# A planned attention and mixer kernel: low parts and sign products from GpSimd to VectorE, with a new order of steps

## The chip, the cores and the metric

The kernel runs on one core of a Trainium2 chip. The metric is the device time of one execution in microseconds. Three runs of the kernel before gave 651.3, 648.9 and 648.49 us; their median is 648.9 us. Engines are named as the profile names them: PE is TensorE, DVE is VectorE, ACT is ScalarE, POOL is GpSimd, and SP is the engine that issues every DMA here.

## The reference

Four batches of 768 tokens go through three stages. The first is a gated linear attention with 8 heads of 48 channels:

```
for t in range(S):
    state = alpha[:, :, t, :, None] * state + einsum('bhd,bhe->bhde', k[:, :, t], v[:, :, t])
    y[:, :, t] = einsum('bhd,bhde->bhe', q[:, :, t], state)
```

The second mixes tokens and channels (`x` is the attention's output, 384 channels wide):

```
theta = x @ w_theta
y = w_tok_r @ (x * cos(theta)) + w_tok_i @ (x * sin(theta))     # over tokens, each batch
u = x + y
x = u + maximum(u @ w_ch, 0)
```

The third is a gated feed-forward: `h = relu(x @ w_in)`, one half of `h` is normalised and mixed over tokens by `w_spatial`, the other half multiplies it, and the result goes through `w_out`. Five of the six weight matrices come as 64-bit floats; `w_spatial` is 32-bit.

## The kernel before

**Units.** A batch is cut into 6 units of 128 tokens, 24 units in all, numbered u = 0 to 23. A unit goes through a chain over four engines: VectorE scans the decays (`att_scan`, two scans and a reciprocal, L451 to L455) and scales keys and queries (`att_kh` L463, `att_qh` L470); PE multiplies them (`att_a` L482, `att_k` L499, `att_u` L515); VectorE masks (`att_mask` L489) and carries the state from half to half (`att_s` L524, `att_t` L537); SP moves the state to another tile by DMA (`move_s` L529); PE forms the output (`att_y` L549), ScalarE copies it (`att_x`), PE transposes it (`tr_p` L568), and the product with `w_theta` follows in two parts (`th_p`, L591 and L594). VectorE reduces the angle (`th_r` L602), ScalarE takes sine and cosine, VectorE multiplies by x (`z_m` L620). Then comes the token mixing: `tokmix(u, m, ri)`, six steps of six matmuls for each unit (L652), which sum over the batch's six units in PSUM.

**High and low parts.** Matmuls of the mixer run on a reduced float type, so that each operand is split into a high part (a rounded copy, made by ScalarE: `z_h` L624, `high` L355 and L357) and a low part, the difference (`z_l` L629 for the activations, `low` L364 for weights, L366 for scaled ones). Three products, high by high, high by low and low by high, make one full product.

**Weight pieces.** The 64-bit weights are turned into 32-bit floats on the chip, in pieces of 128 x 384. `conv` plans the steps of one piece: SP loads it (`raw_f64` L313, two buffers), ScalarE or VectorE takes the sign apart (`sgn` L319 or L321, then `sign` L341), VectorE joins the two halves of the bits (`bits` L329, `join` L336), ScalarE takes the magnitude (`mag` L344), the product with the sign follows (`mul` L349), then `high` and `low`. There are 54 pieces, numbered n: 0 to 2 are `w_theta`, 3 to 26 the two token weights (four pieces for each unit of a batch), 27 to 29 `w_ch`, 30 to 53 the third stage. So the token weights are converted during the first batch, and stay.

**Which engine.** Three numbers share this work between VectorE and GpSimd. `MULP = 3` gives every third piece's sign product to GpSimd (14 of the 42 pieces that have one), `LOP = 2` gives it the low parts of two pieces in four (26, w_theta left out), and `ZLP = 6` the activation low parts of the first six units. Besides, GpSimd only clears four tiles at the start and takes 24 small powers in the third stage.

**Order.** No engine's order is written by hand. Each piece of work is a step with an engine, a cost, predecessors and the buffers that it takes; `latest()` gives it a time, worked back from due times of the token mixing, plus an offset by the step's name (`OFF`, and `OFF0` and `OFF3` for units of the first and last batch). `order()` places the steps on engines by these times, and the program is emitted in the order that comes out, for all engines. Each engine then runs its own steps strictly in that order; SP does too, so a DMA whose buffer is not yet free holds up all DMAs behind it. PSUM has three rotating buffers for all of these products.

Of the kernel before, what the change touches and what calls it, by code (L numbers as in the profile page):

```python
# [40 lines left out]
TH = S // 2  # L41
T0 = 512
OFF = {
# [6 lines left out]
    "sgn": -23.49, "mag": 39.17, "mul": -72.53, "high": -59.59, "low": 17.5, "v": -1.84, "vr": 121.16, "vb": 138.25,  # L50
    "vw": -48.53, "vm": 45.12, "vh": -80.17, "vl": 72.49, "g_u": -21.79, "g_r": -32.74, "g_s": -40.03, "g_m": -104.87,
    "g_h": -88.37, "g_l": 5.15, "o_p": -6.46, "o_e": 26.76, "x2h": 78.95, "x2l": 23.69, "x2": -32.84,
}
SLACK = 1.5
START = 30.0
# [1 line left out]
CHT = 10.6  # L57
CHD = 3.0
LEAD = 1
LOP = 2  # L60
RAWB = 2
OFF0 = {
# [5 lines left out]
}  # L68
OFF3 = {
# [5 lines left out]
}  # L75
SGA = 3
MULP = 3
ZLP = 6
QHB = 2
AMB = 2  # L80
SSB = 2
# [137 lines left out]
def attention_mixer_kernel(  # L219
# [150 lines left out]
    def conv(src, part, key, tiles=(), scale=None):  # L370

        n = len(cvs)
        c = {"src": src, "a": src.shape[1], "part": part, "scale": scale}
        cvs.append(c)
        pool = scale is None and n % 4 < LOP
        c["eng"] = nc.gpsimd if pool else nc.vector
        before = [raws[-1]] if raws else []
        raw, sg, cv = ("raw", RAWB, n), ("sg", 2, n), ("cv", 2, n)
        if src.dtype == I64:
            k0 = step(OFF["raw"], "dma", 1.6, raw_f64, n, after=before, tiles=[raw, *tiles])  # L380
            raws.append(k0)
            k1 = step(OFF["sgn"], *(("act", 0.54) if n % 4 < SGA else ("dve*", 0.27)), sgn, n, after=[k0], tiles=[raw, sg])
            k2 = step(OFF["bits"], "dve*", 0.27, bits, n, after=[k0], tiles=[raw, cv])
            k2 = step(OFF["bits"], "dve*", 0.47, join, n, after=[k2], tiles=[raw, cv])
            k3 = step(OFF["sgn"], "act", 0.52, sign, n, after=[k1], tiles=[sg])
            c["mulp"] = n % MULP == MULP - 1
            k2 = step(OFF["mag"], "act", 0.42, mag, n, after=[k2], tiles=[cv])
            k = step(OFF["mul"], *(("pool*", 0.96) if c["mulp"] else ("dve*", 0.47)), mul, n, after=[k3, k2], tiles=[sg, cv])
        else:
            k = step(OFF["raw"], "dma", 0.8, raw_f32, n, after=before, tiles=[cv, *tiles])  # L390
            raws.append(k)
        k = step(OFF["high"], "act", 0.41, high, n, after=[k], tiles=[cv, *tiles])
        k = step(OFF["low"], *(("pool*", 0.96) if pool else ("dve*", 0.47)), low, n, after=[k], tiles=[cv, *tiles])
        conv_done.setdefault(key, []).append(k)

    wt = {}
# [351 lines left out]
    x2 = {}  # L748
# [144 lines left out]
    for u in range(NU):  # L893
# [21 lines left out]
        ksc = at("sc", "dve*", 2.7, att_scan, after=[kal, prev("att_scan")], tiles=[al, rt])  # L915
        kkh = at("kh", "dve*", 0.6, att_kh, after=[ksc, kqk], tiles=[qk, rt, kh])
        kqh = at("q", "dve*", 0.6, att_qh, after=[ksc, kqk], tiles=[qk, al, qh])
        ka = at("A", "pe", 1.15, att_a, after=[kkh, kqh], tiles=[kh, qh, ps("a")])
        km = at("m", "dve", 0.6, att_mask, after=[ka, ("load_cst",)], tiles=[ps("a"), am])
        k = at("K", "pe", 0.4, att_k, after=[kkh, ("load_cst",)], tiles=[kh, ps("k")])  # L920
        kkt = at("kt", "act", 0.42, att_kt, after=[k], tiles=[ps("k"), kt])
# [2 lines left out]
        kms = []  # L924
        ktx = ("att_t", u - 1, 1) if i else None
        for c in range(2):
# [5 lines left out]
                kms.append(at(f"ms{c}", "dma", 0.3, move_s, c, after=[k, prev("att_y", back=2)], tiles=[*ss, sd]))  # L932
            if not (final and c):
                ktx = at(f"t{c}", "dve", 0.27, att_t, c, after=[k, ku], tiles=[ps("u", c), ("tmp", 1, (u, c)), *ss])
        ky = at("Y", "pe", 1.3, att_y, after=[kqh, km, kvt, *kms], tiles=[qh, am, sd, vd, ps("y")])
        kx = at("x", "act", 0.375, att_x, after=[ky], tiles=[ps("y"), x])
        kp = at("P", "pe", 0.33, tr_p, after=[kx, prev("th_p", 1)], tiles=[x, ps("t")])
        kxh = at("xh", "act", 0.375, tr_h, after=[kp], tiles=[ps("t"), xh])
        kxt = at("xt", "act", 0.375, tr_t, after=[kp], tiles=[ps("t"), xt])
        kxl = at("xl", "dve", 0.46, tr_l, after=[kxh], tiles=[xh, ps("t")])  # L940
# [188 lines left out]
```

## Time and profile before

| what | value |
|---|---|
| median of three runs | 648.9 us |
| profiled execution, its own time | 648.46 us |
| its span, first to last instruction | 646.7 us |
| PE busy | 600.4 us, 93% |
| DVE busy | 431.3 us, 67% |
| ACT busy | 283.4 us, 44% |
| POOL busy | 79.2 us, 12%, 78 instructions |
| DMA, share of 16 engines' span | 31.6% |

1.8 us of the profiled execution lie outside the span. Busy shares are averages over very different stages: PE is busy in 1, 4, 7 and 6 tenths of the page's first four slices (16 us each) and in nine tenths or more from the eighth on. PEclk, the granted TensorE clock, is 7 to 9 tenths in slices three to five and again a little under full in the sixth and seventh, and full after that.

### The profile page before, as it was taken

To read this page: it belongs to the slowest core of one execution; us is meant where nothing else is said; L and a number is where in the kernel's file an instruction comes from. 1 tells how busy PE (TensorE), PEld (TensorE's weight loads), DVE (VectorE), ACT (ScalarE), POOL (GpSimd) and SP (SyncE) were. 2 spreads that over 40 slices of the span, in tenths; PEclk is the share of its full clock that TensorE was granted. 3 is DMA by queue.
4 is the path that set the end of the run, shared out by engine and by line. 5 is a ranking of instruction groups with operands and counts; after the bars stand their busy time and mean duration, and the time that the engine had idled before them with its cause. 6 is when DMAs were issued, how large, how long until landed. Compare 5 with 4: busy or idle time off the path is not lost.

```text
span 646.7 us, 13064 instructions
## 1 busy us (share of the span) xinstructions
PE 600.4 (93%) x5364; PEld 560.2 (87%) x5364; DVE 431.3 (67%) x779; ACT 283.4 (44%) x544; POOL 79.2 (12%) x78
## 2 busy tenths in 40 slices
PE   1476697999999999999999999999999999999997
PEld 1465586788888889988888999999999999999997
DVE  6978988799878787777867768684536533563331
ACT  3357677675234353332448744462423331333122
POOL 1023253241000000000001122220100010010000
PEclk9987999999999999999999999999999999999999
DMA  7766644542532243342224464320100010001002
GB/s 200 203 186 185 186 135 135 152 119 61 155 116 74 79 119 98 104 116 77 60 77 133 131 218 144 139 98 1 50 25 0 14 38 25 1 13 50 13 1 73
DMA packets 41147, 61.46 MB, mean 95 GB/s; under 512 B 4864, under 2 KB 30720, under 8 KB 40576
## 3 DMA queue, kind: packets, MB, share of 16 engines
q1 hardware_dynamic: 41088, 60.64, 31.6%
q8 instruction: 42, 0.69, 0.4%
q14 instruction: 17, 0.14, 0.1%
HBM read 47.94 MB, written 9.44 MB: 89 GB/s over the span
## 4 chain that ended last, share of the span: by engine, by line
PE 85%; DMA 5%; DVE 4%; ACT 3%; SPq 1%; issue 1%; POOL 0%; DVEq 0%; ACTq 0%; POOLq 0%
PE acc L652 22%; PE sp L833 15%; PE psv L776 8%; PE pu L818 8%; PE po L862 8%; PE psc L689 6%; PE psy L549 6%; PE th L591 4%; PE psa L482 3%; PE psu L515 2%; DMA raw<-in_w_theta 2%; PE th L594 2%; DMA raw<-in_w_tr 1%; PE psk L499 1%; DMA sd<-ss 1%; PE pst L568 1%
## 5 line engine op out<-in xcount | busy, mean ns | idle before, releaser
L652 PE MATMUL acc<-w,zs 128*128 128x512 f32 (+1 forms) x864 | 174.7, 347 | 0.0
L652 PEld LDWEIGHTS acc<-w,zs 128*128 128x128 f32 x864 | 135.0, 190 | 18.2 <-issue 0.2
L833 PE MATMUL sp<-w,vns 128*128 128x384 f32 x576 | 105.0, 336 | 0.0
L833 PEld LDWEIGHTS sp<-w,vns 128*128 128x128 f32 x576 | 99.9, 188 | 0.0
L849 ACT CAST gs<-t 128x384 fp32r<-128x384 f32 x32 | 16.3, 513 | 99.1 <-DVE t L843 94.4
L818 PE MATMUL pu<-xs,w 128*128 128x384 f32 x288 | 55.7, 337 | 0.0
L776 PE MATMUL psv<-w,xs 128*128 128x256 f32 x432 | 55.5, 283 | 0.0
L842 DVE TENSOR_TENSOR t<-sp,bsb 128x384 f32<-128x384 f32 x32 | 17.8, 557 | 55.5 <-PE sp L833 55.0
L776 PEld LDWEIGHTS psv<-w,xs 128*128 128x128 f32 x432 | 54.5, 191 | 0.2
L862 PE MATMUL po<-w,gs 128*128 128x384 f32 x288 | 53.0, 336 | 0.0
L818 PEld LDWEIGHTS pu<-xs,w 128*128 128x128 f32 x288 | 50.8, 188 | 0.0
L862 PEld LDWEIGHTS po<-w,gs 128*128 128x128 f32 x288 | 49.8, 188 | 0.0
L349 POOL TENSOR_TENSOR wf<-wf,sg 128x384 f32<-128x384 f32 x14 | 17.6, 1259 | 245.9 <-ACT wf L344 244.3
L549 PE MATMUL psy<-sd,qh 112*64 112x96 f32 x352 | 36.7, 262 | 11.8 <-DMA sd<-ss 5.1
L482 PE MATMUL psa<-qh,kh 48*64 48x64 f32 x768 | 30.2, 233 | 17.2 <-DVE kh L463 16.5
L482 PEld LDWEIGHTS psa<-qh,kh 48*64 48x64 f32 x768 | 26.8, 145 | 22.2 <-DVE kh L463 17.0
L689 PE MATMUL psc<-us,wch 128*128 128x256 f32 x324 | 43.3, 284 | 0.0
L689 PEld LDWEIGHTS psc<-us,wch 128*128 128x128 f32 x324 | 40.9, 190 | 0.9
L549 PEld LDWEIGHTS psy<-sd,qh 112*64 112x64 f32 x352 | 24.9, 143 | 17.0 <-issue 7.4
L364 POOL TENSOR_TENSOR w<-wf,w 128x384 fp32r<-128x384 f32 x24 | 28.7, 1198 | 68.8 <-ACT w L355 68.7
L549 PE MATMUL psy<-vd,am 128*64 128x96 f32 x384 | 36.7, 263 | 0.0
L455 DVE TENSOR_TENSOR_SCAN al<-al,heads 112x536 f32<-112x536 f32 x24 | 34.2, 1423 | 0.8
(83 smaller groups left out, 962.3 us busy)
## 6 DMA issues: line engine op xcount, KB each, us to landing
qk<-in_qka SPq DMA_DIRECT2D x24, 448.0 KB, 4.3
al<-in_qka SPq DMA_DIRECT2D x24, 234.5 KB, 3.0
vd<-in_vt SPq DMA_DIRECT2D x48, 96.0 KB, 2.5
raw<-in_w_tr SPq DMA_DIRECT2D x12, 384.0 KB, 4.0
raw<-in_w_ti SPq DMA_DIRECT2D x12, 384.0 KB, 3.7
x2d<-xT SPq DMA_DIRECT2D x12, 384.0 KB, 3.1
x<-x2d SPq DMA_DIRECT2D x4, 1152.0 KB, 5.2
out<-o SPq DMA_DIRECT2D x24, 192.0 KB, 1.9
```

The lines of the kernel that those rows point to most:

```text
L364: c["eng"].tensor_tensor(out=c["part"](1), in0=f, in1=h, op=ALU.subtract)
L455: nc.vector.tensor_tensor_scan(out=line, data0=line, data1=one, initial=0.0, op0=ALU.mult, op1=ALU.add)
L482: nc.tensor.matmul(psa[o0:o0 + 64, a, c, :], kh[r0:r0 + D, a, c, :], qh[r0:r0 + D, a, c, :], start=True, stop=True,)
L549: nc.tensor.matmul(psy[64 * c:64 * c + 64, a, :], w[:, a, c, :], v[:, c, :, a, :], start=part == 0 or first, stop=part == 1,)
L591: nc.tensor.matmul(th, xh[:, 0, k], wth[:, pr, k], start=(k == 0 and pr == 0), stop=False)
L652: nc.tensor.matmul(acc[b, n][:, c0:c1], zs[:, pl, ri, m * 128:(m + 1) * 128], w[:, pr, t0:t1], start=first and n != 1, stop=last, skip_gro ...
L689: nc.tensor.matmul(ps, wch[:, pl, k, m * 128:(m + 1) * 128], us[:, pr, k], start=(n == 0), stop=(n == 3 * KD - 1),)
L776: nc.tensor.matmul(ps[:, c], xs2[:, pl, k, o:o + 128], w[:, pr, k], start=(n == 0), stop=(n == 3 * KD - 1),)
L818: nc.tensor.matmul(pu, win[f // 2][:, pl, (f % 2) * KD + k], xq[b, h][:, pr, k], start=(n == 0), stop=(n == 3 * KD - 1),)
L833: nc.tensor.matmul(sp[:, :TH], vns[b, s][:, pl, f * 128:(f + 1) * 128], wsp[s][:, pr, h], start=(n == 0), stop=(n == 3 * NS - 1),)
L842: nc.vector.tensor_tensor(out=t1, in0=s2.pop(("sp", b, f, h))[:, :TH], in1=bsb[0][:, t], op=ALU.add)
L862: nc.tensor.matmul(po, gs[b][:, pl, f, s * 128:(s + 1) * 128], wo[f // 2][:, pr, f % 2], start=(n == 0), stop=(n == 3 * KF - 1),)
```

## The change

`MULP = 99`, `LOP = 0` and `ZLP = 0` put every sign product and every low part on VectorE; the 24 powers and the clears are all that GpSimd keeps. All tables of offsets hold new numbers. Two new tables add an offset to all steps of a unit (`UNIT`, units 0 to 8) and to all steps of a weight piece (`PIECE`, pieces 0 to 29). Four of PE's costs in the plan are set anew. No instruction is added or removed, and no buffer changes.

```
-LOP = 2
+LOP = 0
...
+UNIT = {
+    "0": -23.07, "1": -33.34, "2": 6.93, "3": 5.15, "4": 5.03, "5": -20.72, "6": 23.73, "7": -6.29, "8": 22.05,
+}
+PIECE = {
+    "0": 1.03, "1": -60.37, "2": 9.24, "3": -12.69, "4": -92.69, "5": -6.15, "6": -9.14, "7": -95.76, "8": 22.28,
...
-MULP = 3
-ZLP = 6
+MULP = 99
+ZLP = 0
...
+        early = PIECE.get(str(n), 0.0)
...
-            k0 = step(OFF["raw"], "dma", 1.6, raw_f64, n, after=before, tiles=[raw, *tiles])
+            k0 = step(early + OFF["raw"], "dma", 1.6, raw_f64, n, after=before, tiles=[raw, *tiles])
...
-            return step(OFF[name] + more.get(name, 0.0), eng, cost, fn, u, *args, after=after, tiles=tiles, by=by)
+            return step(OFF[name] + more.get(name, 0.0) + UNIT.get(str(u), 0.0), eng, cost, fn, u, *args, after=after, tiles=tiles, by=by)
...
-        ka = at("A", "pe", 1.15, att_a, after=[kkh, kqh], tiles=[kh, qh, ps("a")])
+        ka = at("A", "pe", 1.1, att_a, after=[kkh, kqh], tiles=[kh, qh, ps("a")])
...
-        ky = at("Y", "pe", 1.3, att_y, after=[kqh, km, kvt, *kms], tiles=[qh, am, sd, vd, ps("y")])
+        ky = at("Y", "pe", 1.55, att_y, after=[kqh, km, kvt, *kms], tiles=[qh, am, sd, vd, ps("y")])
...
-        kp = at("P", "pe", 0.33, tr_p, after=[kx, prev("th_p", 1)], tiles=[x, ps("t")])
+        kp = at("P", "pe", 0.3, tr_p, after=[kx, prev("th_p", 1)], tiles=[x, ps("t")])
...
-                    f"T{2 * m + ri}", "pe", 1.08, tokmix, m, ri,
+                    f"T{2 * m + ri}", "pe", 1.1, tokmix, m, ri,
```

In the changed file every line stands 10 or 11 lines further down. The change moves steps on every engine; three places of it follow.

**VectorE, unit 0 at its end.** `z<-z,x` is `z_m(0)`, `zs<-z,zs` the activation's low part, `wf` and `sg` belong to weight pieces. Before, the low part is not in this queue (GpSimd has it):

```order
L463 TENSOR_TENSOR kh<-qk,rt 112x512
L329 TENSOR_SCALAR wf<-raw 128x384
L620 TENSOR_TENSOR z<-z,x 128x768
L470 TENSOR_TENSOR qh<-qk,al 112x512
L336 SCALAR_TENSOR_TENSOR wf<-raw,wf 128x384
L329 TENSOR_SCALAR wf<-raw 128x384
L349 TENSOR_TENSOR wf<-wf,sg 128x384
```

And in the changed kernel:

```order
L631 TENSOR_TENSOR z<-z,x 128x768
L500 TENSOR_TENSOR am<-psa,cst_sb 128x512
L535 TENSOR_TENSOR ss<-tmp,rt 112x192
L359 TENSOR_TENSOR wf<-wf,sg 128x384
L640 TENSOR_TENSOR zs<-z,zs 128x768
L339 TENSOR_SCALAR wf<-raw 128x384
L462 SCALAR_TENSOR_TENSOR rt<-al,heads 112x536
```

The low part now stands four rows behind `z_m(0)` and ahead of unit 4's scan.

**SP, weight pieces 21 to 24.** `raw` is a weight piece, two of `w_tr` and two of `w_ti` for each unit; `sd<-ss` a move of the state, `vd`, `vn`, `al` and `qk` a unit's inputs. Before:

```order
L313 DMA raw<-in_w_ti 128x768
L529 DMA sd_96<-ss 48x192 x2
L313 DMA raw<-in_w_ti 128x768
L442 DMA vd_98<-in_vt 64x2x192 x2
L529 DMA sd_100<-ss 48x192 x2
L313 DMA raw<-in_w_tr 128x768
L428 DMA al<-in_qka 112x536
L313 DMA raw<-in_w_tr 128x768
```

And in the changed kernel:

```order
L323 DMA raw<-in_w_ti 128x768
L447 DMA vn<-in_vn 128x192
L540 DMA sd_96<-ss 48x192 x2
L323 DMA raw<-in_w_tr 128x768
L453 DMA vd_98<-in_vt 64x2x192 x2
L323 DMA raw<-in_w_tr 128x768
L447 DMA vn<-in_vn 128x192
L540 DMA sd_100<-ss 48x192 x2
```

Piece 23, the first `in_w_tr` row of each list, stood behind unit 8's values (`vd_98`) and unit 7's state move (`sd_100`), and stands ahead of both now.

**SP, weight pieces 15 and 16 in the changed kernel.** `al` is unit 9's decays here:

```order
L447 DMA vn<-in_vn 128x192
L439 DMA al<-in_qka 112x536
L323 DMA raw<-in_w_tr 128x768
L443 DMA qk<-in_qka 112x1024
L540 DMA sd_96<-ss 48x192 x2
L540 DMA sd_100<-ss 48x192 x2
L323 DMA raw<-in_w_tr 128x768
```

The load of unit 9's decays takes the buffer that unit 5's scaled queries release, and piece 15 stands right behind it.

## Rows read from the trace of the kernel before

**Rows 1.** Windows: us of the stretch, busy time and count by engine, PEclk, DMA share, GB/s.

```profile
0.00:126.00 126.00, 83.28 (x960) 72.41 (x961) 102.82 (x190) 74.66 (x149) 37.25 (x31) 0.92 0.62 173
7.20:140.00 132.80, 97.28 (x1119) 84.33 (x1120) 114.57 (x206) 85.06 (x170) 41.09 (x27) 0.92 0.61 171
126.00:640.00 514.00, 513.74 (x4388) 484.72 (x4387) 328.53 (x590) 207.75 (x394) 41.94 (x48) 1.00 0.25 76
...
380.00:400.00 20.00, 20.00 (x162) 19.83 (x161) 18.15 (x35) 9.54 (x17) 5.06 (x6) 1.00 0.49 162
```

**Rows 2.** Timeline of PE around 140 us: start, us, engine, line, operation, count.

```profile
140.19 2.36 PE L652 MATMUL acc<-w,zs 128*128 128x512 f32 x12
```

**Rows 3.** Timeline of VectorE, five places: start, us, engine, line, operation.

```profile
7.23 0.36 DVE L329 TENSOR_SCALAR wf<-raw 128x384 uint32<-128x384 uint32 x1 [4.88 <-DMA raw<-in_w_theta]
...
32.41 0.55 DVE L364 TENSOR_TENSOR w<-wf,w 128x384 fp32r<-128x384 f32 x1
32.87 0.68 DVE L470 TENSOR_TENSOR qh<-qk,al 112x512 f32<-112x512 f32 x1
...
81.02 2.32 DVE L470 TENSOR_TENSOR qh<-qk,al 112x512 f32<-112x512 f32 x1
...
119.98 0.36 DVE L321 TENSOR_SCALAR sg<-raw 128x384 f32<-128x384 f32 x1 [4.50 <-DMA raw<-in_w_tr]
...
138.33 0.55 DVE L364 TENSOR_TENSOR w<-wf,w 128x384 fp32r<-128x384 f32 x1
```

**Rows 4.** What VectorE waited for, 7.2 to 140 us: total, times, longest.

```profile
DVE sg L321 <- DMA raw<-in_w_tr: 6.0, 3, 4.5
...
DVE xh L581 <- ACT xT L577: 3.0, 3, 1.3
DVE wf L329 <- DMA raw<-in_w_ti: 2.9, 2, 2.7
```

**Rows 5.** VectorE's groups by shape, 7.2 to 140 us: busy us, mean ns.

```profile
L455 DVE TENSOR_TENSOR_SCAN al<-al,heads 112x536 f32<-112x536 f32 x9 | 14.6, 1625 | 0.3
...
L470 DVE TENSOR_TENSOR qh<-qk,al 112x512 f32<-112x512 f32 x9 | 8.6, 958 | 1.0 <-PE psy L549 1.0
L524 DVE TENSOR_TENSOR ss<-tmp,rt 112x192 f32<-112x192 f32 x16 | 7.4, 461 | 0.1
```

**Rows 6.** The same, 160 to 300 us, where GpSimd runs nothing.

```profile
L455 DVE TENSOR_TENSOR_SCAN al<-al,heads 112x536 f32<-112x536 f32 x12 | 15.3, 1275 | 0.4
L451 DVE TENSOR_TENSOR_SCAN rt<-al,heads 112x536 f32<-112x536 f32 x11 | 13.9, 1266 | 0.0
...
L629 DVE TENSOR_TENSOR zs<-z,zs 128x768 fp32r<-128x768 f32 x10 | 9.5, 952 | 0.8 <-ACT zs L624 0.8
L470 DVE TENSOR_TENSOR qh<-qk,al 112x512 f32<-112x512 f32 x11 | 7.6, 689 | 2.2 <-PE psy L549 2.2
...
L524 DVE TENSOR_TENSOR ss<-tmp,rt 112x192 f32<-112x192 f32 x20 | 7.0, 350 | 0.3
```

**Rows 7.** GpSimd's groups, 7.2 to 140 us: busy us, mean ns.

```profile
L364 POOL TENSOR_TENSOR w<-wf,w 128x384 fp32r<-128x384 f32 x12 | 15.0, 1247 | 33.8 <-ACT w L355 33.8
L629 POOL TENSOR_TENSOR zs<-z,zs 128x768 fp32r<-128x768 f32 x6 | 14.0, 2336 | 24.2 <-DVE tmp L537 9.3 <-ACT zs L624 7.8 <-DVE w L364 6.7
L349 POOL TENSOR_TENSOR wf<-wf,sg 128x384 f32<-128x384 f32 x9 | 12.3, 1371 | 34.8 <-ACT wf L344 34.8
```

**Rows 8.** Timeline of GpSimd: the activation low part of unit 1.

```profile
80.81 1.98 POOL L629 TENSOR_TENSOR zs<-z,zs 128x768 fp32r<-128x768 f32 x1 [3.30 <-ACT zs L624]
```

**Rows 9.** Timeline of SP's queue: piece 23 and what stood ahead of it.

```profile
113.42 1.23 SPq L442 DMA_DIRECT2D vd<-in_vt  x2
114.76 1.20 SPq L529 DMA_DIRECT2D sd<-ss  x2
116.06 0.52 SPq L313 DMA_DIRECT2D raw<-in_w_tr  x1
```

**Rows 10.** DMA issues of the page: KB each, median us to landing.

```profile
raw<-in_w_tr SPq DMA_DIRECT2D x12, 384.0 KB, 4.0
```

More of the change, by code (lines that the diff above doesn't have):

```diff
@@ L43 @@
 OFF = {
[6 rows of a table removed]
-    "sgn": -23.49, "mag": 39.17, "mul": -72.53, "high": -59.59, "low": 17.5, "v": -1.84, "vr": 121.16, "vb": 138.25,
-    "vw": -48.53, "vm": 45.12, "vh": -80.17, "vl": 72.49, "g_u": -21.79, "g_r": -32.74, "g_s": -40.03, "g_m": -104.87,
-    "g_h": -88.37, "g_l": 5.15, "o_p": -6.46, "o_e": 26.76, "x2h": 78.95, "x2l": 23.69, "x2": -32.84,
[6 rows of a table added]
+    "bits": 13.81, "sgn": -20.19, "mag": 24.31, "mul": -40.05, "high": -90.87, "low": 27.87, "v": 7.83, "vr": 48.19,
+    "vb": 135.68, "vw": -53.5, "vm": -6.85, "vh": -8.12, "vl": 39.02, "g_u": 1.95, "g_r": 28.87, "g_s": -1.44,
+    "g_m": -128.36, "g_h": -93.78, "g_l": 27.43, "o_p": -17.5, "o_e": 13.27, "x2h": 133.03, "x2l": 44.92,
+    "x2": -127.67,
 }
@@ L59 @@
 LEAD = 1
-LOP = 2
+LOP = 0
 RAWB = 2
 OFF0 = {
[5 rows of a table removed]
[5 rows of a table added]
 }
 OFF3 = {
[5 rows of a table removed]
[5 rows of a table added]
+}
+UNIT = {
+    "0": -23.07, "1": -33.34, "2": 6.93, "3": 5.15, "4": 5.03, "5": -20.72, "6": 23.73, "7": -6.29, "8": 22.05,
+}
+PIECE = {
[4 rows of a table added]
 }
 SGA = 3
-MULP = 3
-ZLP = 6
+MULP = 99
+ZLP = 0
 QHB = 2
@@ L379, in conv @@
         if src.dtype == I64:
-            k0 = step(OFF["raw"], "dma", 1.6, raw_f64, n, after=before, tiles=[raw, *tiles])
+            k0 = step(early + OFF["raw"], "dma", 1.6, raw_f64, n, after=before, tiles=[raw, *tiles])
             raws.append(k0)
[L382 to L385, printed above, removed]
+            k1 = step(early + OFF["sgn"], *(("act", 0.54) if n % 4 < SGA else ("dve*", 0.27)), sgn, n, after=[k0], tiles=[raw, sg])
+            k2 = step(early + OFF["bits"], "dve*", 0.27, bits, n, after=[k0], tiles=[raw, cv])
+            k2 = step(early + OFF["bits"], "dve*", 0.47, join, n, after=[k2], tiles=[raw, cv])
+            k3 = step(early + OFF["sgn"], "act", 0.52, sign, n, after=[k1], tiles=[sg])
             c["mulp"] = n % MULP == MULP - 1
-            k2 = step(OFF["mag"], "act", 0.42, mag, n, after=[k2], tiles=[cv])
-            k = step(OFF["mul"], *(("pool*", 0.96) if c["mulp"] else ("dve*", 0.47)), mul, n, after=[k3, k2], tiles=[sg, cv])
+            k2 = step(early + OFF["mag"], "act", 0.42, mag, n, after=[k2], tiles=[cv])
+            k = step(early + OFF["mul"], *(("pool*", 0.96) if c["mulp"] else ("dve*", 0.47)), mul, n, after=[k3, k2], tiles=[sg, cv])
         else:
-            k = step(OFF["raw"], "dma", 0.8, raw_f32, n, after=before, tiles=[cv, *tiles])
+            k = step(early + OFF["raw"], "dma", 0.8, raw_f32, n, after=before, tiles=[cv, *tiles])
             raws.append(k)
-        k = step(OFF["high"], "act", 0.41, high, n, after=[k], tiles=[cv, *tiles])
-        k = step(OFF["low"], *(("pool*", 0.96) if pool else ("dve*", 0.47)), low, n, after=[k], tiles=[cv, *tiles])
+        k = step(early + OFF["high"], "act", 0.41, high, n, after=[k], tiles=[cv, *tiles])
+        k = step(early + OFF["low"], *(("pool*", 0.96) if pool else ("dve*", 0.47)), low, n, after=[k], tiles=[cv, *tiles])
         conv_done.setdefault(key, []).append(k)
```

35 rows, old and new, of tables (OFF, OFF0, OFF3, PIECE) are left out of this document.

## The prediction

> **What bounds the kernel now.** I read the windows first. Up to 126 us PE is busy for 83.3 of 126.0 us, so it stands idle for 42.7; from 126 to 640 us it is busy for 513.7 of 514.0 [rows 1]. So the time is the moment at which PE stops waiting, plus a fixed amount of work, and the first 126 us are all that this change can shorten. In that part the granted TensorE clock averages 0.92, and 1.00 behind it [rows 1]. Next, who makes PE wait: from 7.2 to 140 us VectorE is busy for 114.6 of 132.8 us, ScalarE for 85.1, GpSimd for 41.1 [rows 1]. VectorE is the nearest to full, and what it waits for is in the list of its waits. I therefore follow VectorE's queue to one point. PE begins, at 140.19 us, the product of unit 5 with its second token weight, at m = 0 [rows 2]; this needs the low part of weight piece 26, which VectorE makes from 138.33 to 138.88 us [rows 3]. By the new order PE has done the same work at this product, and one more besides (below), so the shift of this point is the change in time, as long as PE does not wait later.
>
> **VectorE's work to that point.** An instruction begins about 0.08 us before the one ahead of it ends (the low part at 32.41 lasts 0.55, the next starts at 32.87 [rows 3]), so a step costs its mean less 0.08. Clean means are those between 160 and 300 us, where GpSimd is idle [rows 6]. A low part or sign product of a piece costs 0.46 [rows 3], an activation low part 0.95 less 0.08 = 0.87, a pair of scans with its reciprocal about 2.7 [rows 6]. The old order has 184 steps in this queue up to the low part of piece 26, 99.7 us by these prices; the new one has 210, 115.8 us. The 16.1 us more are 12 low parts and 9 sign products at 0.46 (9.7), five more activation low parts (six in place of one, 4.4), and 2.0 of steps that changed sides, unit 9's scan above all. The 27 that come from GpSimd are those of [rows 7].
>
> **What else lay in the 138.9 us.** The queue starts at 7.23 us [rows 3], and 7.2 + 99.7 = 106.9; the piece was done at 138.9. The missing 32.0 us split in three.
> - Waits: ten rows of VectorE's list add up to 17.0 us, without the wait for the first piece. 9.1 of it are for weight pieces to land, 5.8 for ScalarE, 2.1 for PE and GpSimd; the three largest stand in [rows 4].
> - Stretched instructions: the second scan takes 1.625 us on average against 1.275 (9 times, 3.2 us), the scaled queries 0.958 against 0.689 (9 times, 2.4), the state product 0.461 against 0.350 (16 times, 1.8) [rows 5, 6]; four smaller groups add 4.0. Together 11.4 us.
> - The remaining 3.6 us are gaps too short to be listed.
>
> That the stretch comes from GpSimd is seen at 81.02 us: the scaled queries take 2.32 us, and they end when GpSimd's low part of unit 1, 80.81 to 82.79, is through [rows 3, 8]. With no such work on GpSimd I take the 11.4 us as gone.
>
> The Trainium skill (SBUF — State Buffer, section "SBUF: two separate sides") says that VectorE and GpSimd share one pair of ports under an exclusive lock, and that the loser waits for the other's whole instruction. The row at 81.02 us agrees. Taken for every instruction of GpSimd the rule would hand back up to its whole 41.1 us [rows 1], 29.7 more than the stretched rows; the stretched rows, 11.4, decide here.
>
> **What waits remain.** This is the term with the widest bounds: 0 if every input is early, 17.0 if all stay. Of the 9.1 us for pieces, 4.5 fall on piece 23 at 119.98 us: its load left SP at 116.06, behind unit 8's values, which went at 113.42 once their buffer was free, and behind a state move [rows 3, 9]. In the new order that piece stands ahead of both. The 2.7 us in [rows 4] are piece 6, behind unit 2's values; it too now stands ahead of them. So 7.2 us lose their cause, and I leave 2.0. Of the 5.8 us for ScalarE I leave 2.5, because VectorE has 16.1 us more of its own to do between ScalarE's results; of the rest 0.5. That makes 5.0, nearer the lower bound since the two largest waits are moved.
>
> **The sum.** 7.2 + 115.8 + 3.6 + 5.0 = 131.6 us, against 138.9: 7.3 us earlier. PE followed 1.3 us behind before, and I keep that. Ahead of this product PE now also does the first part of unit 7's theta product, six matmuls, which at the pace of [rows 2] (12 in 2.36) is 1.1 us less to do behind it. Gain: 8.4 us. Behind the point VectorE has little in hand: from the low part of piece 26 to unit 9's activation low part it has 36.3 us of steps in the new order, and PE 36.9 from the same point to the product that needs it. Whatever VectorE waits there beyond 0.6 us, PE waits too; I take off 1.0. The third stage gets 12 low parts and 4 sign products, 7.4 us, spread over some 60 us; PE is full there and VectorE is not the last, so I cost them at nothing, though the cover is thin: 18.15 of 20 us at 380 to 400 us [rows 1]. The offsets of later units and PE's new costs only reorder work under a busy PE: nothing. Net 7.4 us: 648.46 - 7.4 = **641.1 us** on the profiled execution's scale. The median of the runs, 648.9, stands 0.4 above that execution, inside what I can resolve. Each us of wait moves this by one us: 636.1 us at no waits, 653.1 us at 17.0.
>
> **Rivals.**
> 1. *More comes back.* The 3.6 us of short gaps were GpSimd's doing too, and nearly no wait remains (1 us): 641.1 - 3.6 - 4.0 = 633.5 us; 633.5 to 638 as a case. For it: GpSimd's own low parts average 2.34 us against 1.98 in the row shown [rows 7, 8], so the two were in each other's way often. Against it: PE has three PSUM buffers, whose release hangs on several engines. That rule of the Trainium skill points this way. Chance 0.15.
> 2. *The waits stay, in other places.* VectorE waits 9.5 to 16 us, mostly for ScalarE, which has more results due within a shorter time (85.1 us of 132.8 now [rows 1]). Then 645.6 to 652.1 us, no difference that can be told. For it: VectorE's queue is fixed, and any input out of turn stops all of it. Chance 0.13.
> 3. *Slower: the pieces come late.* The place is SP's queue. Piece 15 stands behind the load of unit 9's decays, which must wait for unit 5's scaled queries, VectorE's 104th step; the piece is first used at its 118th. Between them lie 5.6 us of VectorE steps, against two issues (0.5 us each, [rows 9]) and a landing of 4.0 [rows 10]: 5.0, so 0.6 in hand. Twenty pieces, 7 to 26, are fed through two buffers like that. At 0.37 us late for each, the gain of 7.4 is gone; at 0.6 the waits reach 17.0 and the time is 653.1 us. For it: VectorE's sum is 16.1 us longer, so it must lose fewer waits than before only to stay level. Against it: a VectorE with more to do also asks for its pieces later. Chance 0.07.
> 4. *A late bound.* VectorE becomes the last one between 380 and 420 us, where the third stage's pieces and the normalisation meet. At half of the moved 7.4 us it costs 3.7: 644.8 us. Against it: in 126 to 640 us VectorE is busy for 328.5 of 514 [rows 1]. Chance 0.10.
>
> That the change does not do what it says I leave out: in the new order GpSimd holds the clears and the powers alone.
>
> **How the numbers follow.** My forecast (waits of 2 to 9 us, 638 to 645.1 us) gets 0.55. About 0.5%, 3.2 us, is what a measurement of this kernel can tell from no change. Faster than 645.7 us are the forecast, rival 1 and rival 4: 0.80. Rival 2 lies within the bound: 0.13. Rival 3 is beyond it: 0.07. The range from 634 to 648.5 us takes in the forecast, rival 4, nearly all of rival 1 and the better part of rival 2, some 0.85 in all.
>
> **What would show it.** Right: GpSimd's 27 instructions between 7.2 and 140 us are gone; the scaled queries stay at 0.69 us and the second scan near 1.28; VectorE waits less than 3 us in all for pieces to land; unit 5's second token product begins near 133 us; PE's idle time up to 126 us falls by some 8 us. Wrong: the waits of VectorE for ScalarE or for pieces add up to over 12 us in the first 130 us, or PE is idle by more than 1 or 2 us anywhere from 140 to 640 us, or the early PE clock is lower than 0.92 by enough to eat the gain.

## The result and the profile after

Four runs of the changed kernel gave a median of 640.1 us (638.9 to 642.0), four of the kernel before 649.5 us; the ratio is 0.9855, 95% interval 0.9821 to 0.9888. Measured again later beside other kernels it was 0.9856 (0.9835 to 0.9876). So the change makes the kernel faster by 1.4 to 1.5%. The forecast of 641.1 us, its range and its sign held. The profiled execution took 638.91 us, its span is 637.1 us, 9.6 less than before.

First the windows, to be laid beside [rows 1] (us of the stretch, busy time and count by engine, PEclk, DMA share, GB/s; the third ends at 630 since the span is shorter):

```profile
0.00:126.00 126.00, 95.36 (x1095) 80.74 (x1095) 116.87 (x236) 85.78 (x171) 2.96 (x8) 0.99 0.65 183
7.20:140.00 132.80, 108.34 (x1270) 91.40 (x1271) 128.33 (x254) 91.97 (x185) 0.00 (x0) 0.99 0.65 183
126.00:630.00 504.00, 501.25 (x4252) 471.92 (x4251) 319.19 (x590) 197.46 (x371) 13.92 (x24) 1.00 0.24 75
370.00:390.00 20.00, 20.00 (x163) 19.87 (x163) 18.16 (x40) 9.68 (x17) 1.65 (x3) 1.00 0.55 177
```

Up to 126 us PE is idle for 126.0 - 95.4 = 30.6 us where it was 42.7, 12.1 less. GpSimd's 27 instructions are gone, and VectorE is busy for 128.3 of 132.8 us. But from 126 to 630 us PE is idle for 2.75 us, where it had lost 0.3.

What VectorE waited for, 7.2 to 140 us (beside [rows 4]; total, times, longest):

```profile
DVE wf L339 <- DMA raw<-in_w_theta: 5.6, 1, 5.6
DVE wf L339 <- DMA raw<-in_w_ch: 1.1, 1, 1.1
DVE xh L592 <- ACT xT L588: 0.6, 2, 0.4
DVE wf L339 <- DMA raw<-in_w_tr: 0.6, 1, 0.6
DVE r L613 <- ACT kk L609: 0.2, 1, 0.2
```

The first row is the wait for the very first piece. The w_ch row lies behind piece 26; ahead of it 1.4 us are left of the 17.0.

VectorE's groups in the same stretch (beside [rows 5, 6]; busy us, mean ns):

```profile
L466 DVE TENSOR_TENSOR_SCAN al<-al,heads 112x536 f32<-112x536 f32 x10 | 12.8, 1275 | 0.3
L481 DVE TENSOR_TENSOR qh<-qk,al 112x512 f32<-112x512 f32 x10 | 6.8, 684 | 0.0
L535 DVE TENSOR_TENSOR ss<-tmp,rt 112x192 f32<-112x192 f32 x17 | 5.9, 350 | 0.0
```

All three have the durations of [rows 6]: nothing is stretched any more. The point that the prediction followed, on VectorE's and on PE's timeline (start, us):

```profile
126.14 0.55 DVE L374 TENSOR_TENSOR w<-wf,w 128x384 fp32r<-128x384 f32 x1
```

```profile
127.33 3.42 PE L663 MATMUL acc<-w,zs 128*128 128x512 f32 x18
...
133.99 1.29 PE L663 MATMUL acc<-w,zs 128*128 128x256 f32 x6 [1.02 <-ACT x L567]
```

Unit 5's second token product starts at 127.33 us instead of 140.19 [rows 2], 12.9 us earlier. The second PE row is the largest of the new gaps behind it.

### The profile page after: what moved, and what is told of

It reads as the page before. It is cut to its first block, busy times and chain, and to the rows that moved or that the text cites. A ratio compares the mean times of both kernels' runs of the same rounds, so it can differ in the third digit from the quotient of the medians.

```text
span 637.1 us, 13061 instructions
## 1 busy us (share of the span) xinstructions
PE 600.1 (94%) x5364; PEld 555.8 (87%) x5364; DVE 436.1 (68%) x825; ACT 284.2 (45%) x544; POOL 16.9 (3%) x32
## 4 chain that ended last, share of the span: by engine, by line
PE 77%; DVE 15%; DMA 3%; issue 2%; ACT 2%; SPq 0%; POOL 0%; DVEq 0%; ACTq 0%; POOLq 0%
PE acc L663 19%; PE sp L844 16%; PE psv L787 8%; PE pu L829 8%; PE po L873 8%; PE psc L700 6%; PE psy L560 3%; PE psa L493 3%; PE th L602 2%; DVE rt L462 2%; DVE al L466 2%; DVE wf L346 2%; DVE wf L359 1%; PE psu L526 1%; PE th L605 1%
## 5 line engine op out<-in xcount | busy, mean ns | idle before, releaser
L493 PE MATMUL psa<-qh,kh 48*64 48x64 f32 x768 | 29.9, 232 | 19.1 <-DVE qh L481 17.6
L560 PE MATMUL psy<-vd,am 128*64 128x96 f32 x384 | 35.3, 257 | 0.0
L635 ACT CAST zs<-z 128x768 fp32r<-128x768 f32 x24 | 20.0, 833 | 31.7 <-PE acc L663 20.6
L602 PE MATMUL th<-wth,xh 128*128 128x384 f32 x144 | 31.5, 356 | 2.6 <-DVE tmp L548 1.6
L365 ACT CAST w<-wf 128x384 fp32r<-128x384 f32 x48 | 24.4, 510 | 18.5 <-DVE wf L359 13.4
```

The costliest lines, as they stand in the source:

```text
L365: nc.scalar.copy(out=c["part"](0), in_=f)
L493: nc.tensor.matmul(psa[o0:o0 + 64, a, c, :], kh[r0:r0 + D, a, c, :], qh[r0:r0 + D, a, c, :], start=True, stop=True,)
L560: nc.tensor.matmul(psy[64 * c:64 * c + 64, a, :], w[:, a, c, :], v[:, c, :, a, :], start=part == 0 or first, stop=part == 1,)
L602: nc.tensor.matmul(th, xh[:, 0, k], wth[:, pr, k], start=(k == 0 and pr == 0), stop=False)
L635: nc.scalar.copy(out=st[u]["zs"][:, 0], in_=st[u]["z"])
```

## Experiments

Two numbers of each trace are used throughout: the **point** (start of unit 5's second token product at m = 0, read on PE's timeline) and the rest, span minus point.

| run | us, median | ratio [95%] | point | span | rest |
|---|---|---|---|---|---|
| before | 648.9 | | 140.19 | 646.7 | 506.5 |
| a4, old order, all on VectorE | 649.6 | 1.0003 [0.9989, 1.0017] | 140.39 | 647.6 | 507.2 |
| a1, move alone, planned again | 654.8 | 1.0082 [1.0053, 1.0111] | 136.93 | 655.1 | 518.2 |
| a2, tables alone, planned again | 656.1 | 1.0105 [1.008, 1.013] | 135.43 | 654.2 | 518.8 |
| a3, new order, 46 steps on GpSimd | 647.6 | 0.9975 [0.9962, 0.9988] | 134.48 | 646.9 | 512.4 |
| after | 640.1 | 0.9855 [0.9821, 0.9888] | 127.33 | 637.1 | 509.8 |
| after, once more | 639.4 | 0.9856 [0.9835, 0.9876] | 129.23 | 639.0 | 509.8 |
| b1, without the two new tables | 651.6 | 1.004 [1.0015, 1.0066] | 135.94 | 649.2 | 513.3 |
| b2, new order, 6 steps on GpSimd | 641.7 | 0.989 [0.9872, 0.9909] | 132.61 | 641.4 | 508.8 |
| b5, new order, pieces one place later | 657.1 | 1.0126 [1.0109, 1.0143] | 146.96 | 656.4 | 509.4 |
| b3, new order, other start | 637.0 | 0.9813 [0.9794, 0.9833] | 126.57 | 635.9 | 509.3 |
| b4, b3 and signs on ScalarE | 636.2 | 0.9809 [0.9784, 0.9833] | 124.33 | 633.3 | 509.0 |
| c1, b4 and piece 2 earlier | 637.0 | 0.9816 [0.9799, 0.9833] | 124.38 | 633.9 | 509.5 |
| c2, c1 and two loads later | 636.2 | 0.9806 [0.9785, 0.9826] | 124.47 | 634.1 | 509.6 |

The rest compares runs of one order only: in each order other steps of PE stand ahead of the point. Against the old order the new one has one more there, the first part of unit 7's theta product; a1 has two fewer than the old order, a2 two more token products and one step less, b1 three more than the new order.

### The two halves of the change apart (a1, a2)

In a1 the kernel before gets the new engines and keeps its tables of offsets; the planner orders anew. In a2 the changed kernel gets the old engines.

```diff
-LOP = 2, MULP = 3, ZLP = 6        (a1, in the kernel before)
+LOP = 0, MULP = 99, ZLP = 0
-LOP = 0, MULP = 99, ZLP = 0       (a2, in the changed kernel)
+LOP = 2, MULP = 3, ZLP = 6
```

> The kernel before with the 46 steps on VectorE and nothing else: the old offsets, planned again. Theory 1 (VectorE's queue sets the time; the move frees it of 11.4 us of stretch and costs 15 us of work; what pays is that the new offsets leave no waits): VectorE has 114.9 us of steps up to piece 26's low part, and keeps some 8 to 12 us of waits, so that the point falls at 132 to 136 us and the time is 644 to 648 us. Rival 2 (freeing GpSimd is the gain, the order is a detail): waits under 3 us, 639 to 642 us. Rival 3 (the waits do not change with the engine): 17 us, 650 to 653 us. GpSimd has no instruction between 7 and 140 us in any case, and the scaled queries take 0.69 us.

> The changed kernel with the 46 steps back on GpSimd, planned again with the new offsets and tables. Theory 1: 96.4 us of VectorE steps up to piece 26's low part, 11 us of stretch, and waits of 10 to 20 us because each result of GpSimd comes late and the offsets were not made for it: 643 to 652 us. Rival 2 (freeing GpSimd is the gain): no better than before, 648 to 652 us. A third reading (the order is all of it, the engine does not matter): waits under 3 us, 636 to 641 us.

Both came out slower than before, and slower than everything that was expected of them. Neither half is worth anything by itself, in an order that the planner makes for a mixture that the offsets weren't made for. In a1 the point itself is 3.3 us earlier, and all of that and more is lost in the rest (window of 126 to 640 us):

```profile
126.00:640.00 514.00, 507.97 (x4340) 477.07 (x4339) 329.08 (x612) 203.36 (x383) 14.46 (x24) 0.99 0.25 76
```

PE is idle for 6.0 us there, against 0.3 in [rows 1], at a granted clock a little under full. Since the planner moves everything at once in these two, they don't tell the cost of the engine from that of the order. The next two do.

### The engine alone, in either order (a4, a3)

```diff
 # a4: the order of the kernel before, word for word
-        eng = nc.gpsimd if c["mulp"] else nc.vector      (mul; low and z_l alike)
+        eng = nc.vector
 # a3: the changed kernel's order, word for word
-        eng = nc.gpsimd if c["mulp"] else nc.vector
+        eng = nc.gpsimd if n % 3 == 2 else nc.vector
-        c["eng"] = nc.gpsimd if pool else nc.vector
+        c["eng"] = nc.gpsimd if scale is None and n % 4 < 2 else nc.vector
-        eng = nc.gpsimd if u < ZLP else nc.vector
+        eng = nc.gpsimd if u < 6 else nc.vector
```

> Exactly the order of the kernel before, with GpSimd's 46 steps run by VectorE at their places in it. VectorE has 114.6 us of steps up to piece 26's low part. Theory 1: the stretch is gone, but the order was not made for this queue: waits of 8 to 14 us, 644 to 650 us. Rival 2: waits under 3 us, 639 to 642 us. Rival 3: waits stay at 17 us, 651 to 654 us.

> Exactly the order of the changed kernel, with the 46 steps run by GpSimd at their places in it. VectorE's own work to piece 26's low part falls from 115.8 to 100.9 us. Theory 1: the stretch returns (11 us, 0.42 us for each of 27 instructions, so nearly all that the shorter queue saves), and PE and VectorE wait for GpSimd's 1.2 to 2.3 us results that stood 0.5 to 0.9 us away: 642 to 650 us. If the order is all of it: 7.9 + 100.9 + 11.4 + 3 = 123 us at the point and 634 to 638 us.

In the old order the move is worth nothing: 1.0003. The stretch is gone there too (VectorE's groups of a4, 7.2 to 140 us):

```profile
L455 DVE TENSOR_TENSOR_SCAN al<-al,heads 112x536 f32<-112x536 f32 x9 | 11.5, 1275 | 0.3
L470 DVE TENSOR_TENSOR qh<-qk,al 112x512 f32<-112x512 f32 x9 | 6.2, 685 | 0.0
L524 DVE TENSOR_TENSOR ss<-tmp,rt 112x192 f32<-112x192 f32 x16 | 5.6, 353 | 0.1
```

but the 11.4 us given back, and 3.5 us fewer waits (13.5 for 17.0), are just what the steps cost VectorE, some 15. Most waits stay, those for pieces above all (VectorE's waits in a4, same stretch):

```profile
DVE sg L321 <- DMA raw<-in_w_tr: 5.2, 3, 3.7
...
DVE wf L329 <- DMA raw<-in_w_ti: 2.6, 2, 1.5
DVE xh L581 <- ACT xT L577: 2.1, 3, 0.9
```

In the new order the same steps on GpSimd cost 647.6 against 640.1 us. a3's groups, 7.2 to 140 us, VectorE and then GpSimd:

```profile
L466 DVE TENSOR_TENSOR_SCAN al<-al,heads 112x536 f32<-112x536 f32 x10 | 14.7, 1472 | 0.3
...
L535 DVE TENSOR_TENSOR ss<-tmp,rt 112x192 f32<-112x192 f32 x16 | 6.9, 434 | 0.0
...
L500 DVE TENSOR_TENSOR am<-psa,cst_sb 128x512 f32<-128x512 f32 x9 | 6.1, 678 | 0.0
...
L331 DVE TENSOR_SCALAR sg<-raw 128x384 f32<-128x384 f32 x6 | 3.9, 652 | 0.0
```

```profile
L374 POOL TENSOR_TENSOR w<-wf,w 128x384 fp32r<-128x384 f32 x12 | 16.6, 1388 | 30.0 <-ACT w L365 30.0
L640 POOL TENSOR_TENSOR zs<-z,zs 128x768 fp32r<-128x768 f32 x6 | 12.7, 2124 | 16.1 <-ACT zs L635 16.0
```

The stretch is back (L331, an instruction with one input, takes 0.652 us where it takes 0.352 in the profile after; L500, which reads PSUM, keeps its length), VectorE waits 2.9 us for ScalarE's weight parts instead of nothing, and PE's list of waits has 2.4 us for `zs` from GpSimd. So, of these two orders and two choices of engine, the gain needs both: of 9.4 us, some 1.6 come with the order alone (a3 against before, 0.25%), the other 7.8 when the steps then leave GpSimd. Both runs fell where their first theory had them.

### Are the two new tables needed? (b1)

`UNIT` and `PIECE` are emptied, the rest of the changed kernel stays, and it is planned again.

> The changed kernel with both new tables empty (no offsets for single units or weight pieces), planned again; all steps stay on VectorE. The order then has 217 instead of 209 VectorE steps ahead of the 27th low part (one more set of bits, join, sign, scaled key and query, mask, residue, z and its low part, some 5 us by their durations). Theory that the order of VectorE's queue sets the time: the low part ends 5 us later plus 0 to 4 us of new waits, PE has up to 3 us more done by then, so 642 to 648 us. Rival, that the three main tables of offsets are what counts and the two new ones do nothing: 639 to 641 us.

651.6 us, worse than the worst expected and 11.5 us above the changed kernel: without the two tables nothing of the gain is left. Whether other main tables could do without them was not tried. VectorE's queue isn't starved here (its waits, 7.2 to 140 us, without the first piece, add up to 4.5 us; the largest two are shown), it makes other things first:

```profile
DVE wf L352 <- ACT wf L347: 1.4, 2, 1.1
DVE wf L332 <- DMA raw<-in_w_tr: 1.0, 1, 1.0
```

The low part of piece 26 then ends at 135.3 us, 8.6 later than in the changed kernel, 5 of which are the eight more steps ahead of it; the rest grows by 3.5 us as well, although PE has three steps more done at the point. One place stands out: from 383.85 to 388.07 us PE waits for 3.7 us, most of it here:

```profile
386.40 0.50 PE L693 MATMUL psc<-us,wch 128*128 128x256 f32 x2 [2.56 <-ACT us L677]
```

VectorE is busy for 9.60 of the 10 us from 380 to 390. In this order the late bound of the prediction's rival 4 does occur.

### One kind of step on GpSimd (b2)

```diff
-        eng = nc.gpsimd if u < ZLP else nc.vector
+        eng = nc.gpsimd if u < 6 else nc.vector
```

> Exactly the changed kernel's order on every engine; only the 6 low parts of the decay factor z of units 0 to 5 run on GpSimd. Theory that an instruction on GpSimd costs VectorE nearly as much in stretched neighbours as it saves: VectorE's queue loses 6 x 0.96 us of work and gains about 0.28 us per us of GpSimd's 11 to 12 us, so the low part of piece 26 ends 0 to 2.5 us earlier, and the hand-over to GpSimd (1.9 us instead of 0.96) makes PE wait for zs in 1 or 2 places: 638.5 to 641.5 us. Rival 1, that the stretch comes with the mul and low steps alone: VectorE 5.7 us earlier, 635 to 637 us. Rival 2, that the hand-over of z's low part is the costly one of the 46: 643 to 646 us.

(The `z` of this run is the mixer's activation, the angle's sine and cosine times x; it is no decay factor.) 641.7 us, just above the first theory's span, by another sum: VectorE has 5.7 us less to do, and yet the low part of piece 26 ends at 132.0 us, 5.3 *later* than in the profile after (3.4 later than in its second one). Of these 11.0 us, 2.8 are more gaps of over 0.15 us (4.2 for 1.4) and 7.0 are stretch; 1.2 were not placed. The medians, 641.7 and 640.1 us, lie closer together than the two traces, which are of executions of 643.18 and 638.91 us. The six instructions show the stretch well, because they stand alone. Three of them on GpSimd's timeline, and VectorE's beside them:

```profile
49.26 2.34 POOL L640 TENSOR_TENSOR zs<-z,zs 128x768 fp32r<-128x768 f32 x1 [45.77 <-ACT zs L635]
...
93.14 2.37 POOL L640 TENSOR_TENSOR zs<-z,zs 128x768 fp32r<-128x768 f32 x1 [13.09 <-ACT zs L635]
103.57 2.10 POOL L640 TENSOR_TENSOR zs<-z,zs 128x768 fp32r<-128x768 f32 x1 [8.06 <-ACT zs L635]
```

```profile
49.84 2.90 DVE L462 TENSOR_TENSOR_SCAN rt<-al,heads 112x536 f32<-112x536 f32 x1
...
93.92 0.21 DVE L465 RECIPROCAL al<-rt 112x8 f32<-112x8 f32 x1
94.16 2.47 DVE L466 TENSOR_TENSOR_SCAN al<-al,heads 112x536 f32<-112x536 f32 x1
...
104.42 0.56 DVE L613 SCALAR_TENSOR_TENSOR r<-kk,th 128x384 f32<-128x384 f32 x1 [0.46 <-ACT kk L609]
104.89 0.35 DVE L546 COPY tmp<-psu 112x192 f32<-112x192 f32 x1
105.37 0.72 DVE L359 TENSOR_TENSOR wf<-wf,sg 128x384 f32<-128x384 f32 x1
```

The scan at 49.84 ends at 52.74: GpSimd's end, 51.60, plus nearly its own 1.27. The one at 94.16 does the same (96.63, against 95.51). In the third case two instructions that read PSUM (`th`, `psu`) run through GpSimd's at their usual length, and the sign product behind them, both inputs in SBUF, loses only the last 0.17 us. So it went each of the six times; VectorE lost 1.63, 1.33, 1.21, 1.20, 0.17 and 1.50 us, 1.2 on average, for a step that it does itself in 0.95 [rows 6]. For this step GpSimd is no help but a loss. The Trainium skill (SBUF — State Buffer, section "SBUF: two separate sides") says that a VectorE instruction with two inputs in SBUF, or in a two-port mode, and a GpSimd instruction that reads SBUF lock each other out for the whole instruction. All six cases agree: each instruction that was held has two inputs in SBUF. The reciprocal at 93.92, all in SBUF but with one input, is not held: 0.21 us, its usual length. Rival 1 of this run, a stretch from the other two kinds alone, falls, and so does rival 2: the hand-over is not the costly one.

### Pieces one place later on SP's queue (b5)

The prediction had argued on the places of two pieces. Here 22 of the 24 pieces 3 to 26 go behind the DMA that followed them; no compute engine's order changes.

```diff
+        for n in range(26, 2, -1):
+            i = keys.index(("raw_f64", n))
+            d = [j for j in range(i + 1, len(keys)) if steps[keys[j]][1] == "dma"][0]
+            if d < min(keys.index((f, n)) for f in ("bits", "sgn") if (f, n) in keys):
+                keys.insert(d, keys.pop(i))
```

> The changed kernel's order on the compute engines, but 22 of the 24 weight pieces 3 to 26 are issued on SP's queue behind the load or state move that followed them. Theory of the prediction, that the places of the pieces in SP's queue set VectorE's waits for them: each piece lands at least 0.4 us later, some 1 to 3 us where the overtaking issue has to wait, so VectorE's waits for pieces grow from 1.7 us (ahead of 126 us, without the first piece) to 6 to 12 us and the time to 643 to 649 us. Rival, that the pieces have slack (many are issued when their buffer comes free, not when SP gets to them): waits up by less than 2 us, 639.5 to 641.5 us.

657.1 us, 17.6 above the changed kernel beside it, more than any theory expected. What SP waited for, 7.2 to 140 us, in the changed kernel and in b5:

```profile
SPq L323 <- DVE wf L346: 22.9, 9, 5.7
SPq L453 <- PE psy L560: 12.6, 7, 3.3
SPq L439 <- DVE qh L481: 6.8, 6, 2.1
```

```profile
SPq L453 <- PE psy L560: 19.4, 6, 6.0
SPq L439 <- DVE qh L481: 14.5, 5, 7.7
SPq L447 <- PE psu L526: 9.3, 6, 2.7
...
SPq L323 <- DVE wf L346: 7.9, 2, 6.0
```

In the changed kernel SP mostly stands at a piece (L323) until VectorE frees the buffer, so the piece leaves at the first possible moment. In b5 it stands at a value load (L453), a decay load (L439) and so on, which wait for a unit to be through, and the piece behind them waits along though its buffer is free. VectorE and ScalarE get it late (their waits in b5, 3 to 150 us; the last row is ScalarE's largest):

```profile
DVE wf L339 <- DMA raw<-in_w_ti: 5.9, 5, 2.9
...
DVE sg L331 <- DMA raw<-in_w_tr: 3.5, 2, 2.6
DVE zs L640 <- ACT zs L635: 2.7, 3, 1.6
DVE wf L339 <- DMA raw<-in_w_tr: 2.0, 1, 2.0
```

```profile
ACT sg L329 <- DMA raw<-in_w_ti: 15.1, 8, 2.9
```

VectorE's gaps of over 0.15 us ahead of the low part of piece 26 grow from 2.6 us (the changed kernel beside it) to 17.9, its work stays (117.0 and 118.0), and the point is 17.7 us later. The time follows the point one to one.

### A better start (b3, b4, c1, c2)

In the changed kernel VectorE stands idle until 7.91 us, and is nearly gap-free after. b3 loads unit 0's decays first and scans them ahead of the first piece; the two value loads, which wait for GpSimd's clears, go behind.

```diff
+        first = [
+            ("acc_zero", 0), ("load_al", 0), ("raw_f64", 0), ("load_al", 1), ("raw_f64", 1), ("load_qk", 0),
+            ("att_scan", 0), ("load_vt", 0), ("load_vt", 1),
+        ]
+        for key in first + [k for k in keys if k not in first]:
```

> The changed kernel's order, but at the start the decay rates of unit 0 are loaded first and its scan stands ahead of the first weight piece on VectorE, and the two value loads, which wait for GpSimd to clear their buffers, stand behind the first query and key load. Theory that VectorE's queue alone sets the time up to the 27th low part: VectorE starts at about 4 to 4.5 instead of 7.9 us, its work is gap-free after, so the low part ends 2.5 to 3.5 us earlier and the time is 636.5 to 638.5 us. Rival, that the next pieces and ScalarE are late as well, so the start only moves the wait: 639 to 641 us.

637.0 us. VectorE starts at 3.65 us, 4.3 earlier, but its gain at the low part of piece 26 is 0.8 us against the profile after and 2.7 against its second one. b3's timeline of VectorE shows where some of it went:

```profile
3.65 1.27 DVE L462 TENSOR_TENSOR_SCAN rt<-al,heads 112x536 f32<-112x536 f32 x1 [1.30 <-DMA al<-in_qka]
...
15.59 0.36 DVE L339 TENSOR_SCALAR wf<-raw 128x384 uint32<-128x384 uint32 x1 [1.53 <-DMA raw<-in_w_theta]
```

The third piece now comes 1.5 us too late. So both theories hold in part. b4 also puts the six sign steps of VectorE on ScalarE:

```diff
-        if n % 4 < SGA:
+        if n < 27 or n % 4 < SGA:
```

> As the run with the new start, and the sign steps of every fourth weight piece (6 up to piece 26) on ScalarE instead of VectorE at the same place in the order. Theory that VectorE's queue sets the time and ScalarE, busy 92 of the 133 us up to there, has room: 6 x 0.35 = 2.1 us off VectorE, 1 to 2 us below the run with the new start alone (635 to 637 us). Rival, that 0.63 us more on ScalarE for each of these pieces comes back as waits of VectorE for sg, magnitude or high part: 0 to 3 us above that run.

In the trace the point is 2.2 us earlier than in b3, as VectorE's work says (2.1); the medians, 637.0 and 636.2, are too close to tell. c1 and c2 move loads in the first 40 us; besides the lines shown, their list `first` has `load_vn` of unit 0 and the load of the constants in place of `load_vt` of unit 1:

```diff
 # c1: piece 2 ahead of unit 1's scan, unit 1's value loads ahead of piece 3
+            (("raw_f64", 2), ("att_scan", 1)), (("load_vt", 1), ("raw_f64", 3)), (("load_vn", 1), ("raw_f64", 3)),
 # c2: that, and the decay loads of units 3 and 5 behind
+            (("load_al", 3), ("load_qk", 3)), (("load_al", 5), ("load_qk", 3)),
```

> As the run with the new start and the sign steps on ScalarE, with the third weight piece issued as soon as its buffer is free (ahead of unit 1's value loads). In that run VectorE started 4.2 us earlier than in the changed kernel, but 2.0 us of it went into waits ahead of 16 us. Theory that the place of these loads in SP's queue causes the waits: 0.5 to 1.5 us come back, 634.5 to 636 us. Rival, that the first 20 us are bounded by what the DMA engines move (219 to 236 GB/s in the first three slices), so that another load is late instead: 636 to 637.5 us.

> As the run before it, with the decay rates of units 3 and 5 (234.5 KB each, which the order loads ahead of the fourth weight piece from w_tr's second on) moved behind the first state move. Theory that the DMA engines' rate bounds the start: 0.5 to 2 us below the run before it, as pieces 4 and 5 land sooner. Rival, that VectorE has no wait left there: equal within 0.5 us.

> The changed kernel itself once more, on the same chip as the three runs beside it, so that steps of 1 to 4 us can be told: 639 to 641 us.

c1 and c2 equal b4 within what can be told, with the point at 124.4 and 124.5: for c1 the rival's time, for c2 the equal case. That the DMA engines' rate is the reason, as c1's rival says, was not shown. Why the 1 to 2 us of other waits appear in place of those removed was not followed further. c1 and c2 beat both kernels: their intervals lie wholly below that of the changed kernel measured beside them. b3 and b4 were not measured beside it. The best is some 1.9% below the kernel before.

## Why the prediction was right, step by step

**The method.** "The time is the moment at which PE stops waiting, plus a fixed amount of work." For runs of one order the table bears this out more sharply than the prediction had reason to claim: with the changed kernel's order and nothing on GpSimd, the rest is 509.0 to 509.8 us in seven traces whose points lie 22.6 us apart. But the fixed amount belongs to one order: 506.5 and 507.2 us for the old one, 513 to 519 us for three newly planned ones. A forecast that compares two orders must price the rest too.

**VectorE's work, 115.8 us: held.** 7.91 + 115.8 = 123.7; the low part ended at 126.7, which leaves 3.0 us for waits and short gaps, and 1.4 of it are listed waits.

**The stretch, 11.4 us gone: held**, by the durations at L466, L481 and L535. The sentence on the Trainium skill's rule weighed it as if every instruction of GpSimd could cost its whole length (41.1 us). By b2 a GpSimd instruction costs VectorE what is left of it when VectorE comes to an instruction with two inputs in SBUF: 7.0 of 12.5 us there, 11.4 of 41.1 in the kernel before. So the rule was right, and so was taking the size from the stretched rows. The row at 81.02 us was read a little off: it ends at 83.34, not with GpSimd's instruction (82.79) but 0.55 us behind, nearly its own 0.69, as the held ones of b2 do.

**The waits, 5.0 us: too high.** Measured 1.4, in the second profile 2.6 by its gaps. The reason given, pieces ahead of value loads on SP's queue, is borne out by b5, though that is not the old order: with 22 pieces one place later VectorE's gaps return, to 17.9 us, and 11.4 of them are listed waits for pieces. What was left for ScalarE (2.5) shrank to 0.8.

**Short gaps, 3.6 us kept: too high.** 1.6 in the first profile, 2.8 in the second (121.2 us from the first piece to the end of the low part, less 115.8 and 2.6). Rival 1 had them as a result of GpSimd's work; a4 speaks against that, for GpSimd does nothing there, and 131.5 - 114.6 - 13.3 = 3.6 us of them stay. What shortens them was not tested by itself.

**The start:** VectorE began 0.7 us later (7.91, in the second profile 7.35); the prediction had taken 7.2.

**The point.** 132.9 forecast (131.6 and a lag of 1.3), 127.33 measured (lag 0.6). In the second profile it is 129.23, so executions of one kernel differ by 2 us here. Of the 5.6 us between forecast and first profile, waits are 3.6, short gaps 2.0, the lag 0.7, and the start takes 0.7 back. Rival 1's sum would have put the point at 125.3; both profiles lie between it and the forecast.

PE does not wait at the point, in either kernel. The last waits of over 0.15 us ahead of it are both for the theta product (before, then after):

```profile
125.05 1.34 PE L591 MATMUL th<-wth,xh 128*128 128x384 f32 x6 [1.30 <-ACT xh L572]
```

```profile
124.98 1.34 PE L602 MATMUL th<-wth,xh 128*128 128x384 f32 x6 [0.64 <-ACT xT L588]
```

From there PE runs without such a gap to 140.19 us before and to 127.33 us after; piece 26's low part had been done for 1.3 and 0.6 us. In a1 and a3 the product even begins 0.1 and 0.5 us before that low part is done. So the low part tells how far VectorE's queue has come, but it is not what releases PE, and the "lag" that the prediction kept was other work of PE.

**Behind the point, 1.0 us lost: too low, and the largest error.** 12.9 us earlier plus 1.1 us of work already done make 14.0; the span fell by 9.6. So 4.4 us were lost: 2.5 are more gaps of PE (2.7 for 0.3), the largest ending at 133.99, 213.79 and 252.24 us; 0.4 is the tail after PE's last matmul; 1.5 are left, slightly longer steps by the sum, not traced further. Of the gaps only the first, 1.02 us, lies where the prediction saw little in hand, and by the profile it ended with a copy of ScalarE, not with VectorE. The others, 1.7 us in all, lie in later units and in the third stage, whose new order the prediction put at nothing. The errors ran against each other: 12.9 for 7.3, and 4.4 for 1.0. That the forecast of 641.1 us came so near the median of 640.1 is in part luck.

**The third stage at nothing: held.** PE is full from 370 to 390 us with VectorE at 18.16 us, as in [rows 1]; rival 4 did not occur. One gap of PE, 0.4 us at 442 us, is all there is. That it did not occur hangs on the order: in b1 it did.

**The signs.** GpSimd idle, scaled queries at 0.684 us, second scan at 1.275, waits for pieces under 3 us: all as named. PE's idle time up to 126 us fell by 12.1, not 8. PE's clock rose from 0.92 to 0.99, where a fall was the danger. And "PE idle by more than 1 or 2 us anywhere from 140 to 640 us" nearly came true in sum (1.7 us, the longest gap 0.76), without undoing the result.

**Rivals 2 and 3.** Neither occurred, yet both mechanisms are real. The old order with the same engines (a4) is rival 2: waits stay, no difference. b5 is rival 3: pieces that stand behind one more DMA cost about 0.8 us each (17.7 us for 22), where the prediction had put break-even at 0.37. What kept them away is the new order, not the engine: with all steps on VectorE, a4 keeps 13.5 us of waits in the old order, and b1, planned without the two new tables, has 4.5.

**The range.** It was said to hold the better part of rival 2; of 645.6 to 652.1 us it holds 2.9 of 6.5, under half. The sum of 0.85 stands with that.

## What to carry to other kernels

Work taken off an engine that slows its neighbour may be worth nothing alone: price what the neighbour gets back against what it must now do (11.4 us against some 15 here), and expect the gain from the waits that a new order removes. In a strictly ordered DMA queue, a transfer that only waits for a buffer must stand ahead of those that wait for long chains; one place can cost more than its own issue. To compare two orders, mark the same step in the bound engine's two queues, see what else each has done by then, and price what stands behind it as well.

## What the runs showed of the hardware

- In these runs a GpSimd instruction on SBUF holds a VectorE instruction with two inputs in SBUF until GpSimd is through, and lets one with an operand in PSUM pass: 2.90 us instead of 1.27 at 49.84 us in b2, 0.35 unchanged at 104.89. With one input, in SBUF, both were seen: in a3 L331 is caught (0.652 us on average for 0.352, at most 1.17), and L339 at 111.36 us (2.00 for 0.35); the reciprocals never were (0.21), nor L339 at 49.57 us in b2 (0.35), though GpSimd's instruction had begun at 49.26. What parts these cases was not tested. For the activation low part this makes GpSimd dearer for VectorE (1.2 us) than VectorE itself (0.95).
- The granted clock between 7.2 and 140 us differs by order, from 0.88 in a4 to 0.99 after. In the kernel before, PE did nothing from 106.70 to 110.30 us; then it was granted half the clock (1.2 GHz), and full (2.4 GHz) again from 113.80:

```profile
106.70:110.30 3.60, 0.00 (x0) 0.00 (x0) 3.53 (x4) 2.13 (x5) 3.60 (x2) 1.00 0.43 139
110.40:113.70 3.30, 3.13 (x25) 2.91 (x26) 2.33 (x6) 2.86 (x6) 1.52 (x2) 0.50 0.00 0
```

In b5 the same happened from 101.4 and from 142.4 us on, each time behind 2.40 us in which PE was busy for under 0.1. In the changed kernel, where PE was busy for 14.62 of the 17.40 us from 95.0 to 112.4, it stayed full. How much of the time comes from this was not told apart.

```profile
7.20:140.00 132.80, 99.84 (x1117) 86.40 (x1118) 117.72 (x232) 84.45 (x170) 0.00 (x0) 0.88 0.60 171
```

That is a4; its time was that of the kernel before, which had 0.92 [rows 1], so there a difference of 0.04 in this stretch went with no difference in time.
